# A spectral filter and a two-layer product in float32: the second product with tokens on partitions, and another opening

## The chip, the cores and the metric

The kernel runs on one core of a Trainium2 chip. The time is that of the device, in microseconds (us), from the first to the last instruction of one execution. A core has five engines with their own queues: TensorE (PE) for matrix products, whose weight loads (PEld) are recorded by themselves, VectorE (DVE), ScalarE (ACT), GpSimd (POOL) and SyncE (SP), which here only issues transfers. A TensorE instruction holds one operand, up to 128x128, as weights, and streams the other past it column by column; results land in PSUM, from where VectorE or ScalarE fetch them.

## The reference

```python
x: (8, 3008, 256)                       # batch, sequence, channels
X = np.fft.rfft(x, axis=1)
Y = X * (filt_r + 1j * filt_i)[None]    # one complex factor per frequency and channel
y = np.fft.irfft(Y, n=3008, axis=1)
t = y.reshape(24064, 256)               # tokens
h = t @ w_in                            # (256, 2048)
g = np.where(h > 0, h, np.exp(np.minimum(h, 0)) - 1)
out = g @ w_out                         # (2048, 256)
```

All arithmetic is float32. The two weight matrices arrive as 64-bit floats and are converted in the kernel.

## The kernel before

The transform of length 3008 = 47 x 64 is done as matrix products in two factors. For each of 8 batches: six products with x chunks (`a_unit`), a trip through DRAM (`z_write`, `z_read`), eight units that transform, filter and transform back (`b_unit`, `bi_unit`), a second trip through DRAM (`y_write`, `y_read`), and six groups m of tokens (`n_unit`). Group m has four pairs of token rows; the group m=0 holds 7 rows of 64 tokens instead of 8, so that its half is 224 tokens wide where the others have 256.

Both layers multiply 2x2 blocks in seven products instead of eight (a Strassen form): the four blocks of the second operand and of the tokens are combined ahead, and seven products per step are added up behind. d_ff is cut in four quarters q. One step (b, m, q) has seven products of the first layer ("ups") and the seven of the second layer for the step before it ("downs"), interleaved on TensorE. There are 8 x 6 x 4 = 192 steps.

```python
def half(m):
    return 224 if m == 0 else 256

# first layer: weights w_in, tokens moving
def mm(n, key, start):
    ...
    for a in range(2):
        nc.tensor.matmul(banks[key][:, a, 0:h], w_in[q][:, COMBO[n], a, :], y[n], ...)   # L312

# second layer: weights w_out, tokens moving; channels come out on partitions
def down_steps(b, m, q):
    ...
    def step(n):
        i, u = PLACE[n]
        for a in range(2):
            nc.tensor.matmul(po[i][:, u, 0:h], w_out[q][:, COMBO[n], a, :], g[n][:, a, :],   # L385
                             start=q == 0 and a == 0 and n in (1, 3, 6, 4), stop=True, ...)
        if q == 3 and n in (5, 7):
            ...
            nc.scalar.activation(out=t[:, :, 0:h], in_=po[i][:, :, 0:h], func=AXT.Copy)      # L389
            if n == 7:
                nc.vector.tensor_tensor(out=p3, in0=p3, in1=k[0][:, 1, 0:h], op=ALU.add)     # L392
    def tail():
        ...                                     # six additions into c, L403
        cs_[b, m] = c

# transposed afterwards, so that tokens stand on partitions, and stored
def o_unit(b, m):
    c = cs_.pop((b, m))
    for a in range(2):
        ps = psM.tile([P, 2, D], FP32, tag="mx", name="pso")
        o = op.tile([P, 2, D], FP32, ...)
        for u in range(2):
            for dh in range(2):
                nc.tensor.transpose(ps[0:w, u, ts(dh, P)], c[dh][:, ds((2 * a + u) * P, w)], eye)   # L424
        nc.scalar.activation(out=o[:, 0:full, :], in_=ps[:, 0:full, :], func=AXT.Copy)              # L425
        ...                                     # stores
```

The tokens reach the layers by products with 128 columns moving (`n_unit`, the tile psn):

```python
for q, i in enumerate(order(m)):
    nc.tensor.matmul(ps[:, ts(q, P)], t[:, i - 4 * m, ds(dh * P, P)], w[:, i - 4 * m, :], ...)      # L266
```

The weights come in sixteen blocks k (four per quarter: two of w_in, two of w_out). `w_fetch(k)` loads one, `w_convert(k)` makes it float32 with two ScalarE and seven VectorE instructions, and each second block adds four VectorE additions for the combined blocks. The opening (batch 0) works before the two layers have anything to do:

```python
for k in range(2):
    w_fetch(k)
for c in range(NXC):                      # six chunks of x with their tables, all at once
    x_load(0, c, nc.scalar, ...)
nc.gpsimd.memset(ff, 0.0)
...
w_convert(0); w_convert(1)
wait_x(3)
w_fetch(2); w_fetch(3)                    # five buffers for weight blocks
wait_x(5)
for a in range(2):
    f_read_first(ff, a)                   # the filter, behind x
for k in range(4, 7):
    w_fetch(k)
for c in range(NXC):
    a_unit(0, c); z_write(0, c)
for k in range(2, 6):
    w_convert(k); w_fetch(k + 5)
z_read(0, 0); z_read(0, 1)
for g in range(NG + 2):                   # NG = 8
    ...                                   # bi_unit(0, g - 2), b_unit(0, g), z_read, y_write
    if g in CONVERTS:                     # {1: 6, 3: 7, 5: 8, 7: 9, 8: 10, 9: 11}
        w_convert(CONVERTS[g])
    ...
y_read(0, 0); w_convert(12)
... w_fetch of 13, 14, 15
n_unit(0, 0)
```

Conversions 13 and 14 then stand at the end of step 0, and 15 at the end of step 1.

Of the kernel before, what the change touches and what calls it, by code (L numbers as in the profile page):

```python
# [95 lines left out]
def kernel(  # L96
# [14 lines left out]
    id_d = nc.inline_tensor(np.eye(P, dtype=np.float32), name="id_t").ap()  # L111
# [22 lines left out]
    eye = glob.tile([P, P], FP32, name="eye")  # L134
# [7 lines left out]
    xs, tas, tns, t1s, t2s, ss, t3s, t4s, zs, yds, ys, g_of, po_of, cs_ = ({} for _ in range(14))  # L142
# [6 lines left out]
    def x_load(b, c, queue=nc.sync, place=None):  # L149
        t, w = place or (xp.tile([P, XC, D], FP32, tag="xc", name="xc"), tap.tile([P, XC, P], FP32, tag="ta", name="ta"))  # L150
        xs[b, c], tas[b, c] = t, w
        skip = 1 if c == 0 else 0
        if skip:
            nc.gpsimd.memset(t[64:P, 0, :], 0.0)
        queue.dma_start(w, ta_d[:, ts(c, XC), :])
        lo = b * N + c * XC
        nc.sync.dma_start(t[0:64], raw(x, lo, [[N1 * D, 64], [D, XC], [1, D]]))
        hi = b * N + N1 - c * XC - skip
        nc.sync.dma_start(t[64:P, skip:XC, :], raw(x, hi, [[N1 * D, 64], [-D, XC - skip], [1, D]]))
# [13 lines left out]
    def z_write(b, c):  # L173
        if c == 0:
            zs[b] = zp.tile([96, K2 + 1, D], FP32, tag="z", name="z")
        t = t1s.pop((b, c))
        for p in range(4):
            r0 = p * H + c * XC
            nc.sync.dma_start(zs[b][r0:r0 + XC, 0:K2, :].rearrange("n k d -> k n d"), t[p * 32:p * 32 + 32, :, :])
# [11 lines left out]
    def f_read_first(t, a):  # L191


        r = a * 64
        for c, src in enumerate((filt_r, filt_i)):
            nc.gpsimd.dma_start(t[r:r + 24, :, c, :, :].rearrange("q g u d -> q g (u d)"),
                                raw(src, 2 * a, [[64 * D, 24], [4 * D, NG], [1, 2 * D]]))
            for u in range(2):
                g0 = 1 if a == u == 0 else 0
                for r0, n in ((24, 16), (40, 7)):  # L200
                    nc.gpsimd.dma_start(t[r + r0:r + r0 + n, g0:NG, c, u, :],
                                        raw(src, 64 * (r0 - 23) - 4 * g0 - 2 * a - u,
                                            [[64 * D, n], [-4 * D, NG - g0], [1, D]]))
            if a == 0:
                nc.gpsimd.dma_start(t[24:48, 0, c, 0, :], raw(src, 32, [[64 * D, 24], [1, D]]))
# [164 lines left out]

    PLACE = {1: (0, 0), 5: (0, 1), 3: (1, 0), 7: (1, 1), 2: (2, 0), 6: (2, 1), 4: (3, 0)}

    def down_steps(b, m, q):
        h = half(m)
        g = g_of.pop((b, m, q))
        if q == 0:
            po_of[b, m] = [psO.tile([P, 2, 256], FP32, tag="po%d" % i, name="po%d" % i) for i in range(4)]
        po = po_of[b, m]
        k = {}

        def step(n):
            i, u = PLACE[n]
            for a in range(2):

                nc.tensor.matmul(po[i][:, u, 0:h], w_out[q][:, COMBO[n], a, :], g[n][:, a, :],  # L385
                                 start=q == 0 and a == 0 and n in (1, 3, 6, 4), stop=True, skip_group_check=True)
            if q == 3 and n in (5, 7):
                t = k[i] = kp.tile([P, 2, 256], FP32, tag="k%d" % i, name="k%d" % i)
                nc.scalar.activation(out=t[:, :, 0:h], in_=po[i][:, :, 0:h], func=AXT.Copy)  # L389
                if n == 7:  # L390
                    p3 = t[:, 0, 0:h]
                    nc.vector.tensor_tensor(out=p3, in0=p3, in1=k[0][:, 1, 0:h], op=ALU.add)  # L392

        def tail():
            if q != 3:
                return
            p1, p5 = (k[0][:, u, 0:h] for u in range(2))
            p35, p7 = (k[1][:, u, 0:h] for u in range(2))
            c = [kp.tile([P, 512], FP32, tag="c%d" % i, name="c%d" % i) for i in range(2)]
            (c11, c12), (c21, c22) = ((t[:, 0:h], t[:, h:2 * h]) for t in c)  # L400

            def add(o, i0, i1):
                nc.vector.tensor_tensor(out=o, in0=i0, in1=i1, op=ALU.add)  # L403

            add(c12, po[2][:, 1, 0:h], p1)
            add(c11, po[2][:, 0, 0:h], p1)
            add(p7, p7, c12)
            add(c12, c12, p35)
            add(c21, po[3][:, 0, 0:h], p7)
            add(c22, p7, p5)  # L410
            cs_[b, m] = c

        return [(lambda n=n: step(n)) for n in DOWNS], tail

    def o_unit(b, m):
        c = cs_.pop((b, m))
        for a in range(2):
            ps = psM.tile([P, 2, D], FP32, tag="mx", name="pso")
            o = op.tile([P, 2, D], FP32, tag="o%d" % a, name="o%d" % a)
            full = 1 if m == 0 and a == 1 else 2  # L420
            for u in range(2):
                w = P if u < full else 64
                for dh in range(2):
                    nc.tensor.transpose(ps[0:w, u, ts(dh, P)], c[dh][:, ds((2 * a + u) * P, w)], eye)  # L424
            nc.scalar.activation(out=o[:, 0:full, :], in_=ps[:, 0:full, :], func=AXT.Copy)  # L425
            if full == 1:
                nc.scalar.activation(out=o[0:64, 1, :], in_=ps[0:64, 1, :], func=AXT.Copy)
            i0, i1 = order(m)[2 * a:2 * a + 2]
            for f in range(2):
                r = o[f * 64:f * 64 + 64]  # L430
                for u, w in ((0, 2),) if i1 == i0 + 1 else ((0, 1), (1, 1)):
                    i = (i0, i1)[u]
                    if f and i == 0:
                        continue
                    n1 = N1 - i if f else i
                    nc.sync.dma_start(raw(out, b * N + n1, [[N1 * D, 64], [-D if f else D, w], [1, D]]), r[:, u:u + w, :])
# [4 lines left out]
    wbufs = list(fbufs)  # L441

    def w_fetch(k):
        q, j = divmod(k, 4)

        wd = wds[k] = wbufs[k % 5 if k < 12 else (2, 0, 1, 2)[k - 12]].bitcast(U32).rearrange("p c u d -> p (c u d)").rearrange("p (a w) -> p a w", w=2)
# [67 lines left out]
    with tc.manual_schedule():  # L514


        CONVERTS = {1: 6, 3: 7, 5: 8, 7: 9, 8: 10, 9: 11}
        with tc.tile_pool(name="boot", bufs=1) as bp:
            ff = bp.tile([P, NG, 2, 2, D], FP32, name="ff")
            wbufs += [bp.tile([P, 2, 2, D], FP32, name="wb%d" % i) for i in range(2)]  # L520
            more = [(bp.tile([P, XC, D], FP32, name="xb%d" % i), bp.tile([P, XC, P], FP32, name="tb%d" % i))
                    for i in range(NXC - XBUFS)]

            def wait_x(c):

                nc.gpsimd.tensor_copy(out=junk[0:1], in_=xs[0, c][0:1, 0, 0:1])

            for k in range(2):
                w_fetch(k)
            for c in range(NXC):  # L530
                x_load(0, c, nc.scalar, more[c - XBUFS] if c >= XBUFS else None)
            nc.gpsimd.memset(ff, 0.0)
            for t, d in ((gb, gb_d), (gr, gr_d), (gi, gi_d)):
                nc.gpsimd.dma_start(t, d)
            w_convert(0)
            w_convert(1)
            wait_x(3)
            w_fetch(2)
            w_fetch(3)
            wait_x(5)  # L540
            for a in range(2):
                f_read_first(ff, a)
            for k in range(4, 7):
                w_fetch(k)
            for c in range(NXC):
                a_unit(0, c)
                z_write(0, c)
            for k in range(2, 6):
                w_convert(k)
                w_fetch(k + 5)  # L550
            z_read(0, 0)
            z_read(0, 1)
            for g in range(NG + 2):
                if g >= 2:
                    bi_unit(0, g - 2)
                if g < NG:
                    b_unit(0, g, ff[:, g])
                    if g + 2 < NG:
                        z_read(0, g + 2)
                if g >= 2:  # L560
                    y_write(0, g - 2)
                if g in CONVERTS:
                    w_convert(CONVERTS[g])
                if g == 1:
                    w_fetch(11)
                if g == 4:
                    w_fetch(12)
                if g in (5, 6):
                    x_load(1, g - 5)
# [5 lines left out]
        w_convert(12)  # L575
        nc.gpsimd.tensor_copy(out=junk[0:1], in_=t4s[0, 0][0:1, 0, 0:1])
        for k in (13, 14, 15):
            w_fetch(k)
        nc.scalar.dma_start(eye, id_d)
        n_unit(0, 0)  # L580

# [8 lines left out]
        for c in range(2, XBUFS):  # L590
            at(c - 2, 0, x_load, 1, c)
        for k in (13, 14, 15):
            at(max(k - 14, 0), 1, w_convert, k)
# [3 lines left out]
        for b in range(B):  # L597
# [20 lines left out]
            for m, (s, place) in enumerate(((20, 0), (25, 1), (29, 1), (32, 0), (36, 0), (40, 0))):  # L618
# [3 lines left out]
                at(t + PER + 4 * m + 5, 0, o_unit, b, m)  # L622
# [54 lines left out]
```

## Time and profile before

| what | value |
|---|---|
| time, median of three runs | 2761.64 us (2761.47 to 2763.48) |
| span of the profiled execution | 2761.7 us |
| mean granted TensorE clock | 0.979 |
| TensorE busy, instructions | 2667.8 us, 13376 |
| VectorE, ScalarE, GpSimd busy | 2017.9, 1332.3, 275.3 us |
| the second product (L385) | 5376 matmuls |
| transposes (L424) | 384 |
| first product of the first layer (L312) starts at | 133.3 us |

A line of the table by groups reads: line of the kernel, engine, operation, tile written and tiles read, shapes, count, busy time and mean length of one, idle time of the engine just before them and what ended it. A busy stretch is the union of records; records of matmuls overlap, as their ends are modelled. A line of the waits reads: engine, tile and line that waited, what it waited for, us in total, times, longest.

### The profile page before, as it was taken

The page shows a single profiled execution, that of the slowest core. Times are in us where ns is not written, and L with a number is a line of the kernel's source. Part 1 is how long each engine was busy: PE and PEld are TensorE (multiplying, and loading weights), DVE is VectorE, ACT ScalarE, POOL GpSimd, SP SyncE. Part 2 cuts the span into 40 slices and gives each one's busy share as a digit, 9 for nine tenths or more (in the row PEclk, how much of TensorE's full clock was granted, in tenths as well). Part 3 has the DMA queues.
Part 4 walks back from the last instruction along what each step waited for, and adds up shares of the span by engine and source line. Part 5 has one row for each costly group of instructions (what it writes and reads, how often), then busy time and mean ns, then how long its engine had stood idle before and what let it go on. Part 6 is the DMA issues. An engine that isn't in the chain of part 4 may idle for free.

```text
span 2761.7 us, 36475 instructions
## 1 busy us (share of the span) xinstructions
PE 2667.8 (97%) x13376; PEld 2281.5 (83%) x13376; DVE 2017.9 (73%) x3427; ACT 1332.3 (48%) x2281; POOL 275.3 (10%) x325
## 2 busy tenths in 40 slices
PE   3689999999999999999999999999999999999998
PEld 1278778987899878998789877898789987899887
DVE  4877877777776777767776787767877677777776
ACT  2244455544455444554454544454454544554544
POOL 4311210002000120001200021000210012000000
PEclk7599999999999999999999999999999999999999
DMA  9644421434114331242313332143321223110100
GB/s 243 180 115 120 106 56 29 118 87 99 43 47 117 77 90 37 72 114 71 78 50 87 87 89 66 37 106 94 98 61 39 72 69 94 37 39 19 25 22 16
DMA packets 141634, 214.51 MB, mean 78 GB/s; under 512 B 25268, under 2 KB 99142, under 8 KB 141456
## 3 DMA queue, kind: packets, MB, share of 16 engines
q1 hardware_dynamic: 122656, 173.60, 24.6%
q0 software_dynamic: 17792, 36.93, 5.5%
q8 instruction: 106, 1.74, 0.3%
q10 hardware_dynamic: 1008, 1.64, 0.2%
q14 instruction: 72, 0.59, 0.1%
HBM read 137.04 MB, written 78.12 MB: 78 GB/s over the span
## 4 chain that ended last, share of the span: by engine, by line
PE 86%; DVE 7%; ACT 3%; DMA 2%; issue 2%; ACTq 0%; DVEq 0%; POOL 0%; SPq 0%
PE po L385 37%; PE pha L312 11%; PE phc L312 11%; PE phd L312 11%; PE phb L312 5%; PE psa L167 3%; PE psn L266 2%; PE psr L211 2%; PE pva L211 2%; PE pso L424 2%; DMA z<-t 1%; DVE g L317 1%; ACT e L323 1%; ACT e L324 1%; DVE c L403 1%
## 5 line engine op out<-in xcount | busy, mean ns | idle before, releaser
L385 PE MATMUL po<-g,wo 128*128 128x256 f32 (+1 forms) x5376 | 1324.2, 375 | 0.0
L385 PEld LDWEIGHTS po<-g,wo 128*128 128x128 f32 x5376 | 1021.4, 190 | 116.2
L323 ACT ACTIVATE e<-g 128x512 f32<-128x512 f32 (+1 forms) x576 | 357.6, 621 | 600.5 <-DVE g L317 600.3
L324 ACT ACTIVATE e<-e 128x512 f32<-128x512 f32 (+1 forms) x768 | 477.6, 622 | 24.4
L312 PE MATMUL pha<-y,wi 128*128 128x256 f32 (+1 forms) x1536 | 396.6, 381 | 9.3 <-ACT g L332 9.1
L317 DVE TENSOR_TENSOR g<-phc,g 128x512 f32<-128x512 f32 (+1 forms) x384 | 259.8, 677 | 197.5 <-PE phc L312 197.5
L328 DVE SCALAR_TENSOR_TENSOR g<-e,g 128x512 f32<-128x512 f32 (+1 forms) x576 | 387.5, 673 | 11.6 <-ACT e L324 11.2
L323 ACT ACTIVATE e<-pha 128x512 f32<-128x512 f32 (+1 forms) x192 | 113.0, 588 | 532.2 <-PE pha L312 532.2
L312 PEld LDWEIGHTS pha<-y,wi 128*128 128x128 f32 x1536 | 285.4, 191 | 93.4 <-ACT t L238 34.3
L317 DVE TENSOR_TENSOR g<-phd,g 128x512 f32<-128x512 f32 (+1 forms) x384 | 261.2, 680 | 86.4 <-PE phd L312 65.7
L328 DVE SCALAR_TENSOR_TENSOR g<-e,pha 128x512 f32<-128x512 f32 (+1 forms) x192 | 129.5, 674 | 259.7 <-ACT e L324 259.7
L227 POOL TENSOR_TENSOR sr<-sr,sp 128x512 f32<-128x512 f32 x64 | 80.9, 1264 | 1303.7 <-DVE sp L225 1303.7
L312 PE MATMUL phc<-ys,wi 128*128 128x256 f32 (+1 forms) x768 | 195.5, 377 | 2.8 <-DVE si L224 2.8
L312 PE MATMUL phd<-y,wi 128*128 128x256 f32 (+1 forms) x768 | 195.2, 377 | 1.3
L312 PE MATMUL phb<-ys,wi 128*128 128x256 f32 (+1 forms) x768 | 194.1, 375 | 0.0
L312 PE MATMUL phc<-y,wi 128*128 128x256 f32 (+1 forms) x768 | 194.0, 375 | 0.0
L312 PE MATMUL phd<-ys,wi 128*128 128x256 f32 (+1 forms) x768 | 193.7, 375 | 0.0
L312 PEld LDWEIGHTS phc<-ys,wi 128*128 128x128 f32 x768 | 145.3, 191 | 24.0 <-issue 8.1
L312 PEld LDWEIGHTS phd<-y,wi 128*128 128x128 f32 x768 | 145.2, 191 | 22.5 <-PE phc L312 6.5
L332 ACT ACTIVATE g<-pha 128x512 f32<-128x512 f32 (+1 forms) x192 | 112.7, 587 | 105.7 <-PE pha L312 105.5
L312 PEld LDWEIGHTS phb<-ys,wi 128*128 128x128 f32 x768 | 146.0, 190 | 17.1 <-issue 0.5
L312 PEld LDWEIGHTS phd<-ys,wi 128*128 128x128 f32 x768 | 145.8, 190 | 16.5
(108 smaller groups left out, 2787.9 us busy)
## 6 DMA issues: line engine op xcount, KB each, us to landing
z<-t SPq DMA_DIRECT2D x192, 128.0 KB, 3.9
t<-z SPq DMA_DIRECT2D x128, 192.0 KB, 3.7
yd<-t SPq DMA_DIRECT2D x128, 192.0 KB, 2.8
t<-yd SPq DMA_DIRECT2D x192, 128.0 KB, 4.2
out_dram<-o SPq DMA_DIRECT2D x176, 128.0 KB, 2.4
xc<-in_x_dram SPq DMA_DIRECT2D x84, 256.0 KB, 4.6
f<-fd POOLq DMA_DIRECT2D x112, 192.0 KB, 3.6
tn<-tn_t SPq DMA_DIRECT2D x48, 256.0 KB, 4.1
```

The lines of the kernel that those rows point to most:

```text
L167: nc.tensor.matmul(ps[:, u, :], w[:, r + u, :], xt[:, r + u, :], start=True, stop=True)
L211: nc.tensor.matmul(ps[:, u:u + w, :], table[k, v, :], rhs[k, u:u + w, :], start=True, stop=True)
L227: nc.gpsimd.tensor_tensor(out=sr, in0=sr, in1=p, op=ALU.subtract)
L266: nc.tensor.matmul(ps[:, ts(q, P)], t[:, i - 4 * m, ds(dh * P, P)], w[:, i - 4 * m, :], start=True, stop=True)
L312: nc.tensor.matmul(banks[key][:, a, 0:h], w_in[q][:, COMBO[n], a, :], y[n], start=start and a == 0, stop=True, skip_group_check=True)
L317: nc.vector.tensor_tensor(out=g[o], in0=i0, in1=i1, op=ALU.add)
L323: nc.scalar.activation(out=e, in_=src, func=AXT.Relu, scale=-1.0)
L324: nc.scalar.activation(out=e, in_=e, func=AXT.Exp, scale=-1.0)
L328: nc.vector.scalar_tensor_tensor(out=g[n], in0=es[n], scalar=1.0, in1=src, op0=ALU.subtract, op1=ALU.max)
L332: nc.scalar.activation(out=g["t1"], in_=mm(1, "a", True), func=AXT.Copy)
L385: nc.tensor.matmul(po[i][:, u, 0:h], w_out[q][:, COMBO[n], a, :], g[n][:, a, :], start=q == 0 and a == 0 and n in (1, 3, 6, 4), stop=True, ...
L424: nc.tensor.transpose(ps[0:w, u, ts(dh, P)], c[dh][:, ds((2 * a + u) * P, w)], eye)
```

## The change

The second product changes roles. Activations g (128 of d_ff by 128 tokens) become the weights, and w_out (128 of d_ff by 128 channels) moves. Tokens so come out on partitions, as the output wants them, and the transposes, their copies and the identity matrix go. A product with 256 tokens needs two such matmuls. In the group m=0, with 224 tokens, the second starts at token 96, so that tokens 96 to 127 are computed twice. The sums are added straight into the tiles that are stored.

At the same time the opening takes another form: four x chunks instead of six at first, three buffers for weight blocks instead of five, the filter's reads behind the third x chunk instead of behind the sixth, and conversions among the x products. The zeroing of ff moves from GpSimd to VectorE, and the DRAM tile z loses one padding row.

```diff
-                nc.tensor.matmul(po[i][:, u, 0:h], w_out[q][:, COMBO[n], a, :], g[n][:, a, :],
-                                 start=q == 0 and a == 0 and n in (1, 3, 6, 4), stop=True, skip_group_check=True)
+                for v, t in enumerate((0, h - P)):
+                    nc.tensor.matmul(po[i][:, u, v, :], g[n][:, a, t:t + P], w_out[q][:, COMBO[n], a, :],
+                                     start=q == 0 and a == 0 and v == 0 and n in (1, 3, 6, 4), stop=True,
+                                     skip_group_check=True)
...
-                nc.scalar.activation(out=t[:, :, 0:h], in_=po[i][:, :, 0:h], func=AXT.Copy)
-                if n == 7:
-                    p3 = t[:, 0, 0:h]
-                    nc.vector.tensor_tensor(out=p3, in0=p3, in1=k[0][:, 1, 0:h], op=ALU.add)
+                nc.scalar.activation(out=t, in_=po[i], func=AXT.Copy)
...
+            o = [op.tile([P, 2, D], FP32, tag="o%d" % i, name="o%d" % i) for i in range(2)]
+            (c11, c21), (c12, c22) = ((t[:, :, 0:P], t[:, :, P:D]) for t in o)
...                                             # seven additions
-            cs_[b, m] = c
+            o_store(b, m, o)
-    def o_unit(b, m):                           # transposes, copies, stores: gone
...
-            zs[b] = zp.tile([96, K2 + 1, D], FP32, tag="z", name="z")
+            zs[b] = zp.tile([96, K2, D], FP32, tag="z", name="z")
...
-        wd = wds[k] = wbufs[k % 5 if k < 12 else (2, 0, 1, 2)[k - 12]]...
+        wd = wds[k] = fbufs[k % FBUFS]...       # FBUFS = 3
...                                             # the opening
-            for c in range(NXC):
-                x_load(0, c, nc.scalar, more[c - XBUFS] if c >= XBUFS else None)
-            nc.gpsimd.memset(ff, 0.0)
+            for c in range(XBUFS):              # XBUFS = 4
+                x_load(0, c, nc.scalar)
+            nc.vector.memset(ff, 0.0)
+            nc.gpsimd.tensor_copy(out=junk[0:1], in_=xs[0, 2][0:1, 0, 0:1])
...
+            w_fetch(2)
+            f_read_first(ff)
             for c in range(NXC):
                 a_unit(0, c)
+                if c + XBUFS < NXC:
+                    x_load(0, c + XBUFS, nc.scalar)
                 z_write(0, c)
-            for k in range(2, 6):
-                w_convert(k)
-                w_fetch(k + 5)
+                w_convert(c)
+                w_fetch(3 + c)
...
-                if g in CONVERTS:
-                    w_convert(CONVERTS[g])
...
+                if g % 2 == 1:
+                    k = 6 + g // 2
+                    w_convert(k)
+                    w_fetch(k + 3)
...
-        w_convert(12)
+        w_convert(11)
...
-        for k in (13, 14, 15):
-            at(max(k - 14, 0), 1, w_convert, k)
+        for k in range(12, 16):
+            at((0, 0, 1, 2)[k - 12], 1, w_convert, k)
```

The first x chunk of batch 1 is loaded behind the first `n_unit` instead of within the loop over g.

## Prediction

> **What bounds the kernel now.** I read the page's first table, then its chain of work that ended last, then the busy time by stretches, then TensorE's waits, and last its timeline, where the spacing of the instructions shows.
>
> ```profile
> PE 2667.8 (97%) x13376; PEld 2281.5 (83%) x13376; DVE 2017.9 (73%) x3427; ACT 1332.3 (48%) x2281; POOL 275.3 (10%) x325
> ...
> PE 86%; DVE 7%; ACT 3%; DMA 2%; issue 2%; ACTq 0%; DVEq 0%; POOL 0%; SPq 0%
> ```
>
> TensorE is busy 97% of the span and makes up 86% of the chain. The stretches say where the other 3% lie (columns: stretch, length, busy us of PE, weight loads, VectorE, ScalarE, GpSimd, then clock, DMA share, GB/s):
>
> ```profile
> 0.00:130.00 130.00, 58.78 (x185) 23.28 (x186) 81.77 (x143) 32.28 (x55) 55.65 (x73) 0.64 0.84 208
> 130.00:300.00 170.00, 158.47 (x777) 141.56 (x777) 126.69 (x221) 78.99 (x139) 30.99 (x35) 0.95 0.49 124
> 300.00:2700.00 2400.00, 2395.76 (x12158) 2068.99 (x12157) 1769.52 (x2996) 1195.36 (x2045) 188.64 (x217) 1.00 0.27 69
> ```
>
> From 300 to 2700 us TensorE idles 4 us in 2400 at full clock: every ns that its stream gains or loses there goes into the span one to one, and work taken from ScalarE (50% there) or VectorE (74%) is worth nothing. Before 130 us it idles 71 us. So there are two questions: how long the new stream is, and whether the other opening gets to the first layer sooner than at about 133 us.
>
> A matmul's recorded length overlaps its neighbour's, so lengths are not to be summed; the distance from one start to the next counts. TensorE's timeline (start, us, line, tile, count):
>
> ```profile
> 182.67 0.92 PE L385 MATMUL po<-g,wo 128*128 128x224 f32 x4
> 183.43 0.92 PE L312 MATMUL pha<-y,wi 128*128 128x224 f32 x4
> ...
> 256.83 1.03 PE L385 MATMUL po<-g,wo 128*128 128x256 f32 x4
> 257.69 1.95 PE L266 MATMUL psn<-tn,t 128*128 128x128 f32 x16
> 259.47 1.03 PE L312 MATMUL phc<-y,wi 128*128 128x256 f32 x4
> ...
> 271.56 1.04 PE L424 MATMUL pso<-eye,c 128*128 128x128 f32 x8
> 272.44 1.03 PE L312 MATMUL phc<-y,wi 128*128 128x256 f32 x4
> ```
>
> Spacing, from start to start: 0.86/4 = 215 ns for 256 columns (216 over longer stretches, 862 ns per four from 1000.12 to 1002.71), 0.76/4 = 189 ns for 224, 1.78/16 = 111.3 ns for 128, and 0.88/8 = 110 ns for a transpose. The 128-column row psn is the model for the new product: float32, a fresh 128x128 weight load before each matmul, 128 moving columns.
>
> Counts: 8 batches x 6 groups x 4 quarters = 192 steps, each 7 products x 2 halves = 14 kernel calls, so 2688; the page has 5376 for L385. One float32 call is thus two hardware matmuls. A transpose call is one (48 x 8 = 384 on record for pso).
>
> **What the Trainium skill says.** "TensorE: Matmul & The Clock Gate", section "Back-to-back issue gap", puts the warm gap at N/2.4 + 2.5 ns for N columns. With N=256 that would be 109 ns; the trace has 216, which is the formula with the columns doubled (512/2.4 + 2.5 = 215.8). Doubled for 128 columns it gives 109.2, and the trace has 111.3. The same page, "LDWEIGHTS (loading the stationary operand)", gives columns/1.2 for a load, 106.7 ns for 128 columns whatever the rows. At 216 ns this hides twice over; at 111 ns load and matmul are nearly equal, which fits the 2 ns over the formula. No run here separates them yet. "Perfetto Trace Analysis", section "Identifying the Most-Contended Engine", says that matmul busy share misleads and weight-load busy is a better sign of how full TensorE is; here that is 83%, and the change doubles the loads of the largest group.
>
> **The change part by part.** (1) The second product. Weights and moving operand change places. Each call with 256 tokens moving becomes two calls with 128 tokens as weights and the 128 columns of w_out moving. L385 goes from 5376 to 10752 hardware matmuls. Before: 4480 x 216 ns = 967.7 us, and 896 of the shorter group (224 tokens) x 189 = 169.3, together 1137.0. After: 10752 x 111.3 = 1196.7. That is +59.7 us, all on the path. It has two terms. For the full groups 8960 x 111.3 - 967.7 = +29.6: two short matmuls cost 222.6 where one long cost 216. For the group m=0 1792 x 111.3 - 169.3 = +30.1: its 224 tokens are now covered by two slices of 128 that overlap by 32, so it does the work of a full group.
>
> (2) The transposes go. 384 x 110 ns = 42.2 us of TensorE. The table by group has 2.0 us of TensorE idle before them. Together -44.2 us. Their ScalarE copies (96 of 584 ns, and 8 small ones) go as well, and a PSUM buffer each; ScalarE has slack, so I count nothing.
>
> (3) VectorE. The same seven additions per group, one of them moved into the tail, now writing the output tile directly. No gain and no loss counted.
>
> (4) The end. In the record of before the last product's matmuls end at about 2753.3, and there follow additions, transposes (to 2755.6), copies (to 2756.3) and four stores. Without transposes and copies the stores start about 1 us sooner, with one addition more ahead of them: -1 us.
>
> Steady part and end: +59.7 - 44.2 - 1 = +14.5 us.
>
> (5) The opening. It goes from six x chunks at once, five weight buffers and filter after x to four chunks, three buffers and the filter after the third chunk. TensorE's waits before 300 us:
>
> ```profile
> PE psr L211 <- ACT wl L472: 31.3, 1, 31.3
> PE psn L266 <- ACT wf L473: 13.0, 1, 13.0
> PE psa L167 <- DMA xc<-in_x_dram: 11.2, 3, 5.6
> PE pha L312 <- ACT g L332: 9.1, 2, 8.8
> ```
>
> The 31.3 us up to 63.6 end with z read back. DMA is full until then (share 1.04 in the first 50 us, 248 GB/s), and in both versions the same bytes of x, tables, filter and z must move before it. Only their order changes, so I expect that point within a few us. Against the new order: weight conversions 2, 3 and 4 now stand in ScalarE's queue between the copies of the x products, and conversion 3 needs a weight block issued behind all filter reads, so the last z write may slip by up to 8 us. For it: before has conversions 0 to 10 ahead of the last inverse product, after 0 to 9. One conversion is 3.65 us of VectorE (119.63 to 123.28 in its timeline) or 5.4 with its four sums, and VectorE is the busiest engine of this stretch (81.8 of 130 us, TensorE 58.8). That is some 5 us sooner. It comes back later: four conversions instead of three are left for the first quarters of the second phase. The 8.8 us wait at L332 is two of them in one quarter; the fourth adds perhaps 4 us. Sum: 0, with a lean of +2 because z's padded row is taken out too and because the opening of before looks like one arranged with care. I take +2, and allow -10 to +12.
>
> Sum: 2761.6 + 14.5 + 2 = 2778 us.
>
> **Rivals.** First, weight loads as the bound: if a fresh load with 128 columns can't be kept at 111 ns over long runs (psn has runs of 16 only; the new stream has 56 such matmuls among 28 long ones per quarter), the new product takes more. On top of my sum, 124 ns would make +137 us and 115 ns +40 us. For it: weight-load busy at 83% already. Against it: psn's 16 in a row show no drift, and the mix leaves (28 x 216 + 56 x 111)/84 = 146 ns per matmul on average.
>
> Second, the gain is real: the spacing is 109 as for transposes, and the second opening is better. Then 10752 x 109.2 = 1174, +37 - 45 = -8, with -8 of opening some 2746. For it: every removed operation stood on the bounding engine. Against it: the load-bound spacing of the only like group.
>
> Third, removing the transposes takes waits with it: a transpose needs VectorE's additions and a shared PSUM buffer. The 2.0 us idle before them and 4 us of idle in 2400 say that there is nothing further to win.
>
> Fourth, the opening decides: a slip of the conversions in three buffers could cost 10 to 20 us, as each fetch now waits for the conversion three before it.
>
> **Range and chances.** The steady term has an error of about 5 us (0.5 ns of spacing is 5.4), the opening about 9. Together some 10, so 8 in 10 lie within about 15: 2763 to 2796, with the upper side longer for the first and fourth rivals. 2% are 55 us. Faster than 2706 would need more than all transposes free and nothing added: chance 0.01. Slower than 2817 needs a spacing of 115 ns or more: 0.05. The rest, 0.94, within 2%.
>
> **What would show it.** In the changed profile: L385 about x10752 with starts 111 ns apart; no pso; in 300 to 2700 us TensorE still idle by 5 us or less; first L312 near 133 us, give or take 10; VectorE and ScalarE shares lower or equal. The prediction is wrong if the spacing in L385 is 109 or over 114 ns, if TensorE shows waits for VectorE or ScalarE in the steady part, or if the first L312 starts over 12 us away from 133.

## The result and the profile after

The changed kernel takes 2794.03 us (median; 2793.49 to 2795.29), the kernel before beside it 2762.14. The ratio is 1.0115, with a 95% interval of 1.0098 to 1.0133: slower by 32 us, about twice the rise of 16 that was forecast, and at the upper end of the stated range. The profile's table of engines and its chain, for the kernel after:

```profile
PE 2687.6 (96%) x18368; PEld 2437.9 (87%) x18368; DVE 2022.9 (72%) x3428; ACT 1288.9 (46%) x2177; POOL 268.4 (10%) x322
...
PE 75%; DVE 13%; ACT 6%; issue 3%; DMA 2%; POOL 0%; DVEq 0%; SPq 0%; ACTq 0%; POOLq 0%
```

TensorE has 4992 matmuls more and is still the bound, but its share of the chain has fallen from 86% to 75%, and VectorE's and ScalarE's have risen from 10% to 19% together. That is the first sign that the new stream waits for them. The steady stretch of the kernel after (columns as in the prediction), and TensorE's waits in it:

```profile
300.00:2700.00 2400.00, 2392.16 (x16564) 2187.03 (x16563) 1749.68 (x2965) 1142.42 (x1928) 192.43 (x221) 1.00 0.27 69
```

```profile
PE phc L310 <- DVE si L222: 4.0, 14, 0.3
PE phc L310 <- DVE g L315: 2.0, 8, 0.3
```

In the steady part TensorE idles 8 us of 2400 instead of 4, although it has more to do, and its waits are all for VectorE: 6.0 us, where the kernel before had 2.8. The first matmul of the first layer starts at 136.0 us instead of 133.3. The new product's two rows in the table by groups:

```profile
L385 PEld LDWEIGHTS po<-wo,g 128*128 128x128 f32 x10752 | 1382.2, 192 | 49.8
L385 PE MATMUL po<-wo,g 128*128 128x128 f32 x10752 | 1386.7, 275 | 0.0
```

The count is the one worked out. The next two fences show the same place in both kernels, in step 57 (batch 2, its step 9); pha to phd are the first layer's PSUM tiles, po the second's, pso the transposes'. TensorE's timeline of the kernel before:

```profile
929.30 1.03 PE L385 MATMUL po<-g,wo 128*128 128x256 f32 x4
930.16 1.04 PE L424 MATMUL pso<-eye,c 128*128 128x128 f32 x8
931.03 1.03 PE L312 MATMUL phc<-y,wi 128*128 128x256 f32 x4
```

And of the kernel after:

```profile
940.24 1.05 PE L385 MATMUL po<-wo,g 128*128 128x128 f32 x8
941.13 1.03 PE L310 MATMUL phc<-ys,wi 128*128 128x256 f32 x4
...
942.86 1.05 PE L385 MATMUL po<-wo,g 128*128 128x128 f32 x8
944.16 1.13 PE L310 MATMUL phc<-y,wi 128*128 128x256 f32 x4 [0.25 <-DVE g L315]
```

Eight of the new matmuls take 0.89 us from start to start where nothing waits (940.24 to 941.13): 111 ns each, as forecast. The next eight, at 942.86, are followed only 1.30 us later. So 0.41 us is lost there, and the record shows 0.25 of it as idle. Before, eight transposes stood in just this place and took 0.87 us; the first layer's phc came at 931.03, when its PSUM bank had meanwhile become free. In this place the new kernel is rid of 0.87 us of transposes, but it waits for 0.41 us.

What VectorE does before that point, in the kernel after:

```profile
939.77 0.75 DVE L400 TENSOR_TENSOR o<-po,k 128x256 f32<-128x256 f32 x2
...
941.90 0.41 DVE L400 TENSOR_TENSOR o<-k,k 128x256 f32<-128x256 f32 x1
942.23 0.69 DVE L315 TENSOR_TENSOR g<-phb,g 128x512 f32<-128x512 f32 x1
...
943.42 0.69 DVE L315 TENSOR_TENSOR g<-phc,g 128x512 f32<-128x512 f32 x1
```

L400 are the seven closing additions of a group: 939.77 to 942.31. The first layer's own addition on phb stands behind them in VectorE's queue, though its matmuls (a group of four that precedes the one at 938.48) were long done; the addition on phc follows at 943.42 and ends at 944.11, and TensorE's next matmul, which adds into the same PSUM bank, starts at 944.16. In the kernel before six of the same additions stand at the same place; the seventh (L392) comes earlier:

```profile
926.45 0.75 DVE L403 TENSOR_TENSOR c<-po,k 128x256 f32<-128x256 f32 x2
...
928.57 0.68 DVE L317 TENSOR_TENSOR g<-phb,g 128x512 f32<-128x512 f32 x1
...
929.77 0.68 DVE L317 TENSOR_TENSOR g<-phc,g 128x512 f32<-128x512 f32 x1
```

There VectorE is done with phc at 930.45, while the transposes (930.16 to 931.03) still occupy TensorE. So the theory to test was: the transposes filled gaps in which TensorE would have waited for VectorE, and their removal is worth less than the time they occupied.

From the starts of the 192 steps (the first L312 or L310 matmul of each) the whole difference can be split. In batch 1, and within 3 ns in batch 3: a step of a full group is 208 ns longer (207 to 211), a step of m=0 956 ns (954 to 957). With these taken off, the removed transposes give back 873, 871, 366, 775, 781 and 547 ns in the batch's steps 1, 5, 9, 13, 17 and 21, together 4.21 us instead of 6 x 0.88 = 5.28. The first and the last batch differ. Batch 7, which has no transform of a next batch beside it, gives back 3.70 us. In batch 0 step 5 is 2.0 us longer instead of 0.66 shorter: three zero-fills of the filter's buffers stand in VectorE's queue behind the additions, and TensorE waits for it 2.5 us where the kernel before waited 1.2 us ahead of its transposes.

### The profile page after: what moved, and what is told of

Its sections match the earlier page's. It is cut to its first block, busy times and chain, and to the rows that moved or that the text cites. A ratio compares the mean times of both kernels' runs of the same rounds, so it can differ in the third digit from the quotient of the medians.

```text
span 2793.5 us, 46413 instructions
## 1 busy us (share of the span) xinstructions
PE 2687.6 (96%) x18368; PEld 2437.9 (87%) x18368; DVE 2022.9 (72%) x3428; ACT 1288.9 (46%) x2177; POOL 268.4 (10%) x322
## 4 chain that ended last, share of the span: by engine, by line
PE 75%; DVE 13%; ACT 6%; issue 3%; DMA 2%; POOL 0%; DVEq 0%; SPq 0%; ACTq 0%; POOLq 0%
PE po L385 34%; PE pha L310 10%; PE phc L310 9%; PE phd L310 9%; PE phb L310 5%; DVE g L315 3%; PE psa L165 3%; ACT e L322 2%; ACT e L321 2%; DVE o L400 2%; PE pva L209 2%; DVE g L326 2%; PE psr L209 2%; PE psn L264 1%; DVE g L359 1%
## 5 line engine op out<-in xcount | busy, mean ns | idle before, releaser
L385 PEld LDWEIGHTS po<-wo,g 128*128 128x128 f32 x10752 | 1382.2, 192 | 49.8
L385 PE MATMUL po<-wo,g 128*128 128x128 f32 x10752 | 1386.7, 275 | 0.0
L310 PE MATMUL pha<-y,wi 128*128 128x256 f32 (+1 forms) x1536 | 397.4, 381 | 7.5 <-ACT g L330 7.4
L310 PEld LDWEIGHTS pha<-y,wi 128*128 128x128 f32 x1536 | 263.0, 191 | 78.8 <-ACT t L236 34.1
L310 PE MATMUL phc<-y,wi 128*128 128x256 f32 (+1 forms) x768 | 196.1, 378 | 5.5 <-DVE g L315 5.0
L310 PE MATMUL phc<-ys,wi 128*128 128x256 f32 (+1 forms) x768 | 195.4, 377 | 4.0 <-DVE si L222 4.0
L310 PE MATMUL phd<-y,wi 128*128 128x256 f32 (+1 forms) x768 | 194.7, 376 | 1.3
L310 PE MATMUL phd<-ys,wi 128*128 128x256 f32 (+1 forms) x768 | 194.8, 376 | 0.0
L310 PE MATMUL phb<-ys,wi 128*128 128x256 f32 (+1 forms) x768 | 194.6, 376 | 0.0
L310 PEld LDWEIGHTS phd<-y,wi 128*128 128x128 f32 x768 | 144.7, 190 | 22.3 <-PE phc L310 6.5
L310 PEld LDWEIGHTS phc<-y,wi 128*128 128x128 f32 x768 | 134.3, 191 | 19.3 <-DVE g L315 8.9
L310 PEld LDWEIGHTS phc<-ys,wi 128*128 128x128 f32 x768 | 131.5, 191 | 14.6 <-issue 6.3
L315 DVE TENSOR_TENSOR g<-phb,g 128x512 f32<-128x512 f32 (+1 forms) x192 | 129.5, 674 | 19.2 <-PE phb L310 18.6
```

The source lines that it names most:

```text
L315: nc.vector.tensor_tensor(out=g[o], in0=i0, in1=i1, op=ALU.add)
L385: nc.tensor.matmul(po[i][:, u, v, :], g[n][:, a, t:t + P], w_out[q][:, COMBO[n], a, :], start=q == 0 and a == 0 and v == 0 and n in (1, 3, ...
```

## The experiments

Times are medians, each beside runs of the kernel before on the same chip (2760.9 for the first four, 2761.7 for the second four, 2762.3 for the last two, 2762.1 beside the changed kernel), so that a difference between rows of different groups, or to the changed kernel, is uncertain by 1 or 2 us.

| run | us | ratio to before (95%) |
|---|---|---|
| old product, transposes left out | 2728.28 | 0.9883 (0.9866 to 0.9899) |
| old product, other opening | 2763.56 | 1.0009 (1.0000 to 1.0017) |
| new product, opening of before | 2792.52 | 1.0114 (1.0098 to 1.0129) |
| changed kernel, additions late | 2771.00 | 1.0039 (1.0024 to 1.0054) |
| old product, additions late | 2766.52 | 1.0017 (1.0010 to 1.0024) |
| changed kernel, slices of 96 tokens | 2773.08 | 1.0046 (1.0028 to 1.0064) |
| changed kernel, m=0 in the old form | 2771.47 | 1.0038 (1.0024 to 1.0052) |
| old product, additions late, no transposes | 2706.84 | 0.9803 (0.9788 to 0.9819) |
| old product, additions late, transposes moved | 2751.67 | 0.9960 (0.9948 to 0.9973) |
| both forms mixed, additions late | 2748.51 | 0.9949 (0.9936 to 0.9963) |

**The transposes alone.** The kernel before, without them and their copies; the output keeps its channels on partitions.

```diff
-                    nc.tensor.transpose(ps[0:w, u, ts(dh, P)], c[dh][:, ds((2 * a + u) * P, w)], eye)
-            nc.scalar.activation(out=o[:, 0:full, :], in_=ps[:, 0:full, :], func=AXT.Copy)
+            o = c[a].rearrange("p (u d) -> p u d", u=2)      # stored as it stands
```

> The kernel before, with the transposes, their ScalarE copies and the identity left out; the sums are stored as they stand, channels on partitions, so the output is not the reference's. Theory (the transposes stood partly in gaps where the next first-layer product had to wait for VectorE anyway): the time falls by 34 us, to 2728. Rival (every transpose costs the 110 ns that it occupies, 42 to 44 us in all): 2718 to 2720.

Measured 2728.28, 33 us less than before: the theory's number and not the rival's. By steps it saves 876 ns in the batch's steps 1, 5, 13 and 17 (875 to 880), but 435 in step 9 and 621 in step 21, 4.56 us together (batch 7: 2.25). TensorE's timeline at the place shown above:

```profile
920.27 1.03 PE L385 MATMUL po<-g,wo 128*128 128x256 f32 x4
921.47 1.13 PE L312 MATMUL phc<-y,wi 128*128 128x256 f32 x4 [0.17 <-DVE g L317]
922.43 1.03 PE L385 MATMUL po<-g,wo 128*128 128x256 f32 x4
```

1.20 us for four matmuls that take 0.86: a new wait for VectorE of 0.34 us where the transposes were, with the old product. So the wait does not need the new product. The new product adds to it: of the 1.05 us per batch that its transposes fail to give back, 0.70 are missing here too (445 ns in step 9, 259 in step 21), and 0.35 are not. The seventh addition, which the change moves into the closing ones, is the likely cause: they hold VectorE for 2.46 us (939.77 to 942.23) instead of 2.12 (926.45 to 928.57). No run moves it alone.

**The opening, from both sides.** The old product with the other opening, and the new product with the opening of before. The edits take `down_steps` and the storing from one kernel and the rest from the other; in words:

```diff
 # old product, other opening: the changed kernel with
-    def down_steps ... o_store            # tokens as weights
+    def down_steps ... o_unit             # w_out as weights, transposes, identity
 # new product, opening of before: the reverse, put into the kernel before
```

> The old second product with its transposes, but the changed opening. Theory (the opening costs the 2 us that the starts of the steps of batch 0 leave over): 2764. Rival (the opening carries the 10 us that the forecast lacks): 2772 or more.

> The new second product without transposes, but the opening of before. Theory: 2792, that is +64 for the product, -34 for the transposes, no opening. Rival (the opening carries 10 us): 2784.

Measured 2763.56, 2.7 us over before with an interval from 0 to 5, and 2792.52, which is 31.6 over the kernel before beside it, where the changed kernel is 31.9 over. Both agree with an opening worth 0 to 3 us and exclude 10. By itself it does not carry the missing time.

**The additions later.** In the changed kernel five of the seven closing additions move into the middle of the next step.

```diff
             add(c12, po[2][:, 1], p1)
             add(c11, po[2][:, 0], p1)
-            add(p7, p7, c12)
-            ...
-            o_store(b, m, o)
+            def behind():
+                add(p7, p7, c12)
+                ...
+                o_store(b, m, o)
+            late_of.append(behind)        # called in the next step, ahead of its plan's first place
```

> The changed kernel with five of the seven closing additions of a group emitted in the middle of the next step instead of at the end of this one, so that the first layer's VectorE work of that step is not behind them. Theory (the additions delay the first layer's VectorE work, and TensorE waits for it in steps 9, 13, 17 and 21 of a batch): the waits go, 8 us less, 2786. Rival (the missing 10 us lie in the product itself or in the opening): 2794, no change.

Measured 2771.00, 23 us less, far more than the 8 expected. By steps, batch 1 is 508 ns shorter in step 9, 859 in 13, 853 in 17 and 326 in 21, 2.55 us together; all others stay within 1 ns. In steps 9 and 21 that is what was missing there (514 and 333); in 13 and 17 it is the missing 105 and 99 and 0.76 us more in each. The eight batches together are 23.1 us shorter, 3.5 of it in step 5 of batch 0. The place shown above, first TensorE, then VectorE:

```profile
932.79 1.05 PE L385 MATMUL po<-wo,g 128*128 128x128 f32 x8
933.68 1.03 PE L310 MATMUL phc<-y,wi 128*128 128x256 f32 x4
```

```profile
929.69 0.75 DVE L400 TENSOR_TENSOR o<-po,k 128x256 f32<-128x256 f32 x2
930.36 0.68 DVE L315 TENSOR_TENSOR g<-phb,g 128x512 f32<-128x512 f32 x1
```

The eight take 0.89 again, and the first-layer addition follows behind two closing additions instead of seven. The theory holds in its mechanism, but the size that I expected was wrong: I had counted only the waits that the change had uncovered. Steps 13 and 17 had others that were there before, and that TensorE's idle time barely shows. There the filter's products (L224) stand behind the closing additions in VectorE's queue, and the first layer waits for the PSUM bank that they empty. This is the kernel before, in step 61 (batch 2, its step 13):

```profile
984.33 1.03 PE L385 MATMUL po<-g,wo 128*128 128x256 f32 x4
985.54 1.10 PE L312 MATMUL phc<-ys,wi 128*128 128x256 f32 x4 [0.19 <-DVE si L224]
986.74 1.10 PE L312 MATMUL phd<-y,wi 128*128 128x256 f32 x4
987.67 1.03 PE L385 MATMUL po<-g,wo 128*128 128x256 f32 x4
```

From start to start these are 1.21, 1.20 and 0.93 us where 0.86 is the pace: 0.76 us lost, with 0.19 shown as idle, since the modelled end of one record reaches into the gap before the next.

**The same in the kernel before**, with the transposes moved one step on, so that they find their sums done.

```diff
-                at(t + PER + 4 * m + 5, 0, o_unit, b, m)
+                at(t + PER + 4 * m + 6, 0, o_unit, b, m)      # and additions late, as above
```

> The kernel before with four of its closing additions in the middle of the next step, and the transposes one step later. Its steps 13 and 17 of each batch show the same waits for VectorE (some 350 ns and 257 ns and slower neighbours, about 1.6 us per batch). Theory (the same additions hold up the first layer here too, only less, because transposes stand in part of the gaps): 13 us less, 2748. Rival (the gaps belong to the tokens-as-weights form alone): 2761.

Measured 2766.52, slower than before by 5 us, neither number. The waits for VectorE are gone, but two new ones stand in steps 2 and 6, 2.1 us longer each than before, where the transposes take 0.88. TensorE's waits of the steady part are now 11.5 us, in twelve places, all for ScalarE. Its timeline in step 50:

```profile
833.57 1.04 PE L427 MATMUL pso<-eye,c 128*128 128x128 f32 x8
835.57 0.70 PE L167 MATMUL psa<-xc,ta 128*128 128x256 f32 x2 [0.96 <-ACT o L428]
```

There the x products follow the transposes and share four PSUM buffers with them and with the first layer; they wait until ScalarE has emptied one. The edit had brought its own collision.

**Slices of 96 tokens.** The changed kernel with 96 weight columns instead of 128; a quarter of the tokens of each slice is left out of the second product and of the output.

```diff
-                    nc.tensor.matmul(po[i][:, u, v, :], g[n][:, a, t:t + P], ...)
+                    nc.tensor.matmul(po[i][0:96, u, v, :], g[n][:, a, t:t + 96], ...)   # additions and stores on 96 partitions
```

> The changed kernel with 96 tokens instead of 128 in every weight slice of the second product; the last 32 tokens of each slice are left out of the second product and of the output. The moving side stays at 128 columns. Theory (at 111.4 ns the weight load of 128 columns is the bound, and the stream alone would take 109.2): the spacing falls to 109 ns, the time by 24 to 27 us, to 2768. Rival (111.4 is the price of any change of weights): spacing and time as in the changed kernel, 2794. In neither does the cost fall with the tokens by a quarter (that would be some 300 us).

Measured 2773.08, 21 us less. The timeline:

```profile
886.69 1.04 PE L385 MATMUL po<-wo,g 128*96 128x128 f32 x8
887.56 1.03 PE L310 MATMUL phb<-ys,wi 128*128 128x256 f32 x4
```

0.87/8 = 109 ns, so the width of the weight slice sets the 111 ns, and 109 comes next, with 128 columns moving in both. The load is the likely part of it: its record is 163 ns long instead of 192. (The transposes load 128 columns too and keep 109; their loads are recorded with 141 ns.) That fits what the Trainium skill says in "TensorE: Matmul & The Clock Gate", "LDWEIGHTS (loading the stationary operand)": the load goes by its columns; its formula gives, as an estimate, 80 ns for 96 and 107 for 128. The records are longer, but differ by about as much (29 ns against 27). A plain step is 125 ns shorter (56 x 2.2 = 123), which is 20 us in the 160 plain steps; steps 9, 13, 17 and 21 gain nothing, as the waits for VectorE take it. A quarter fewer tokens save under 1% of the kernel's time and 2% of a matmul's.

**The group m=0 in the old form.** Both forms of `down_steps` stand in the kernel, and m picks one.

```diff
+    def down_steps(b, m, q):
+        return (down_old if m == 0 else down_new)(b, m, q)
...
+                if m == 0:
+                    at(t + PER + 4 * m + 5, 0, o_unit, b, m)
```

> The changed kernel with the group of 224 tokens (m=0) in the old form, with its transposes; the other groups in the new form. Theory (each of its 32 steps pays 957 ns for the second slice of tokens, and its transposes are worth 0.87 us per batch): 8 x (3.83 - 0.87) = 24 us less, 2770. Rival (m=0 is no dearer than the others, and the loss is spread evenly over the groups): a sixth of 30 us, 2789.

Measured 2771.47, 22.6 us less: one group of six carries most of the loss of 32.

**The transposes once more, without waits.** The old product, additions late, transposes left out (channels on partitions in the output). The edits are those above.

```diff
-                    nc.tensor.transpose(ps[0:w, u, ts(dh, P)], c[dh][:, ds((2 * a + u) * P, w)], eye)
+            o = c[a].rearrange("p (u d) -> p u d", u=2)      # and additions late
```

> The old product with the additions late, and the transposes and their copies left out (channels on partitions, so not the reference's output). Theory (without the waits for VectorE the transposes are worth all that they occupy): 42 us less than the same kernel with transposes, about 2706. Rival (transposes overlap something else as well): 34 us less, 2714.

Measured 2706.84. The kernel to compare with is the next one, in which the transposes collide with nothing.

**The old product, additions late, transposes moved.**

```diff
-                at(t + PER + 4 * m + 5, 0, o_unit, b, m)
+                at(t + PER + 4 * m + 6, 1 if m in (0, 5) else 0, o_unit, b, m)
```

> The old product with the additions late, as in the run before with that, but the transposes of the groups m=0 and m=5 at the end of their step, where no x product asks for the shared PSUM buffers. Theory (that run lost 2.4 us per batch in its steps 2 and 6, where the x products waited for ScalarE to empty the buffers of the transposes, and nothing else): 19 us less than it, 2747, which is faster than the kernel before by 14. Rival (the transposes in the middle of a step delay the first layer wherever they stand): 2760 or more.

Measured 2751.67, 15 us less than with the collision (19 expected) and 10.6 less than before. It is 44.8 us above the same kernel without transposes, about what the forecast took off for them (44.2). Its steps say 5.25 us per batch, six times 875 ns: with no wait behind them the transposes cost all that they occupy. In the kernel before their removal gave 33.

**Both forms mixed.** The same, with the new form in m=1 to 5.

```diff
+        return (down_old if m == 0 else down_new)(b, m, q)
...
+                if m == 0:
+                    at(t + PER + 6, 1, o_unit, b, m)
```

> The same, with the new product (tokens as weights, no transposes) in the groups m=1 to 5 and the old one in m=0. Theory (a full group pays 4 x 208 ns for the shorter matmuls and saves 876 ns of transposes, 44 ns in its favour, 40 times): 2 us less than the old product with late additions, 2745. Rival (the new form is dearer by more than its spacing says): 2755 or more.

Measured 2748.51, 3.2 us under the run above, whose ratio interval it overlaps, and 0.5% faster than the kernel before. By steps it is 0.21 us less per batch, 1.7 in all, as expected: in a full group the new product with its saved transposes is some 40 ns cheaper than the old one, once nothing waits. Its steady stretch:

```profile
300.00:2700.00 2400.00, 2400.00 (x16105) 2202.18 (x16104) 1773.69 (x3010) 1168.20 (x1981) 189.19 (x217) 1.00 0.27 69
```

TensorE shows no idle time in 2400 us.

## Why the prediction was right or wrong

The direction was right and the rise is under 2%, but the size was not right: +16 forecast, +32 found. Batch 1's steps times eight, beside the terms of the forecast:

| term | forecast, us | found, us | from |
|---|---|---|---|
| full groups | +29.6 | +33.3 | 20 steps x 208.3 ns x 8 |
| group m=0 | +30.1 | +30.6 | 4 steps x 956 ns x 8 |
| transposes | -44.2 | -33.7 | 4.21 us x 8 |
| opening and end | +1 | +1.6 | rest of 31.8, the difference of the two recorded spans; what batches 0 and 7 do otherwise stands in it |

**The step that failed** is part (2), "384 x 110 ns = 42.2 us of TensorE", plus 2.0 us of idle time, taken as a gain in full. The occupied time was right: the last pairs of runs give 5.25 us per batch for it. The credit was wrong. In four of a batch's six places 1.05 us of it turned into waits for VectorE (514 ns in step 9, 333 in 21, 105 and 99 in 13 and 17, against 880), and the 2.0 us of idle time were no gain of the transposes' going: 1.2 of them were the one wait for VectorE in batch 0, which passed on to the next matmul and grew to 2.5, and 0.7 the wait for the last additions at the end, which belongs to part (4). The runs with the additions late show it from the other side: they take the waits for VectorE of the steady part away, and there the transposes are worth 44 us. Part (3), which counted no loss for the addition moved into the tail, has a share of some 0.35 us per batch, if that addition is what sets the two forms apart. The third rival named the right pair, transposes and waits, and drew the wrong conclusion, that "there is nothing further to win": it asked whether waits would go with the transposes, not whether they would appear in their place. Of the signs that the prediction named, the one for this came: waits for VectorE in the steady part, and 8 us of idle time instead of at most 5.

**The reading behind it.** "From 300 to 2700 us TensorE idles 4 us in 2400" is true of the records and misled me. The Trainium skill, "Perfetto Trace Analysis", "Tensor Engine Instruction (MATMUL, LD_WEIGHTS)", says that the end of a matmul is computed and not observed; here a matmul of 256 columns is recorded with 379 ns and followed after 216, so 0.16 us of every gap is covered. I used start to start for the pace of the instructions and went back to busy time for the waits. The additions late show what was hidden: in the kernel before 1.51 us per batch in steps 13 and 17 (the old product's gain in the late form) of batches 0 to 6, 10.6 us in all; batch 7 has none.

**Part (1)** had its mechanism right: 111.4 ns, two short for one long, and m=0 paying for a full group. Full groups were 3.7 us dearer. A long group of four behind the short ones takes 866 instead of 863 ns, six times per step, which gives 3 us over all steps; the rest lies in the decimals of the spacing. What sets the 111 ns, which the prediction left open, the slices of 96 tokens narrowed down to the weights' side.

**Parts (4) and (5)** held within a few us: the rest is +1.6, with 2.7 in it from step 5 of batch 0 (2.0 + 0.66), and the runs with exchanged openings at 0.3 to 2.7. The end (4) overlaps with (2): the last eight transposes and the wait ahead of them were counted there. The first layer began 2.8 us later, within the ten allowed. **The first rival** (loads that can't keep 111 ns) and **the second** (109 ns and a better opening) are out by the spacing; **the fourth** by the exchanged openings.

## What to carry to other kernels

Work that is taken from the bounding engine is worth its time only where the next instruction is ready: look at what follows it, and when the other engine's result for that lands. Read waits of a matmul stream from start to start; idle time between modelled ends leaves out part of every gap. And before swapping the two operands of a product, count columns on both sides: here 224 tokens moving took 189 ns against 216 for 256, but as weights a slice of 96 took 109 ns against 111 for 128, so that a partial slice of tokens costs nearly as much as a full one.

## What the runs showed of the hardware

A float32 matmul with 128 moving columns behind a fresh load of 128 columns keeps 111.4 ns in runs of 8 and 16 among long ones, and 109 ns behind loads of 96. Four long ones (256 columns) take 866 ns behind such a run and 863 behind long ones. Moving four or five small VectorE additions of 0.42 us by half a step took 23 us off 2794 in the changed kernel, and in the old one, once the transposes stood free of a PSUM collision, 10.6 off 2762; the change of the product itself, with the transposes it saves, costs some 30.
